# Gate differences taken on 128 partitions, prefix products in two scans, swapped rows put right at the copy of x, and a new order: an mLSTM with two MLP layers on Trainium2

## The chip, the cores and the metric

The kernel runs on one core of one Trainium2 chip. The metric is the device time of one execution in microseconds (us); the median of three runs is given with their lowest and highest. The engines are called PE (TensorE), VectorE (DVE in rows), ScalarE (ACT), GpSimd (POOL) and SyncE (SP, which issues the DMA transfers).

## The reference

Two batches of eight heads with 768 tokens each pass through a recurrent attention (an mLSTM), and its output, as 1536 rows of 320, through two MLP layers with a width of 2048. Everything is to be computed with the accuracy of fp32; the weights of the layers arrive as 64-bit floats.

```python
def _attn_ref(q, k, v, i_gate, f_gate, o_gate):
    ...
    for t in range(S):
        m_new = np.maximum(f_gate[:, :, t] + m, i_gate[:, :, t])
        f_stab = np.exp(f_gate[:, :, t] + m - m_new)
        i_stab = np.exp(i_gate[:, :, t] - m_new)
        m = m_new
        C = f_stab[:, :, None, None] * C + i_stab[:, :, None, None] * np.einsum('bhd,bhe->bhde', vt, kt)
        n = f_stab[:, :, None] * n + i_stab[:, :, None] * kt
        ...
        y[:, :, t] = o * h_tilde / denom
def _moe_ref(x, w_in, w_out):
    h = x @ w_in
    g = h * np.clip(h + 3.0, 0.0, 6.0) / 6.0
    return g @ w_out
def _moe2_ref(x, w_in, w_out):
    h = x @ w_in
    g = h * np.tanh(np.log1p(np.exp(h)))
    return g @ w_out
```

## The kernel before, in words

**Attention.** The 768 tokens are cut into six chunks of 128, each in two halves of 64. `scan_gates` computes the running maximum m for 16 rows (batch and head) by a scan on VectorE (L662) and then, by an addition and two subtractions on the same 16 partitions (tile `gio`; L309 is the helper that every operation on two tensors goes through), the arguments of the two exponentials; it runs for chunk 0, for chunk 1 (its three operations on POOL or VectorE, as the table `pool_scan` says) and for chunks 2 to 5 at once. `gates(c)` transposes the two results to 128 partitions by PE (bank `pg`), and ScalarE and VectorE make the exponentials from two sigmoids (tiles `ist` and `s`). Then it transposes the forget gates to 16 rows, and takes their prefix products over each half by a scan of 128 columns (tile `pr`), for which the first column of each half is copied to `first` and set to zero. `decays` (tile `fb`, two scans of 512 columns per chunk), `scores`, `cross`, `carry` and `within` are the matrix parts. `loads` brings the queries and keys of a chunk (`qke`, one buffer) and its keys, values and output gates (`kvo`). `mixture` ends a chunk: normalising, the output-gate product (`kvo<-fb,kvo`), two "tail" copies on ScalarE (L1034), PE's transposes into bank `xp`, and ScalarE's copies to `x`, the input of the first MLP layer: a rounded part (L1050) and the rest (L1056 or a subtraction on VectorE). For the second batch the two halves of a chunk stand in swapped order in the 128 rows, from `within` to the output.

**Layers.** Each product of the MLP layers is made in three products of high and low parts (`wh`, `wl`, `wd` of the weights, `gh`, `gl` of the activations). The weights of one slice are loaded in 64 bits (`ri` for the up part, `ro` for the down part, four buffers), narrowed to fp32 by a copy on ScalarE (`top`) and an integer operation on VectorE (L367), and split into high and low part by ScalarE and one of VectorE, POOL or PE (bank `pw`, `minus`). Layer 1 (`step1`, `step1_wide`) uses banks `ph` and `acc`, layer 2 (`step2`) `qh` and `bcc`, in three blocks of 512 columns. `store` copies an output tile from its bank and stores 128 rows of 320; for the second batch it does so in two transfers of 64 rows each (L1090), which puts the halves right.

**The order.** All of this is written as tasks that a planner (`Flow`) runs at build time: each step names its engine and a cost, and among those that could start next the one with the lowest number of the table `P` is recorded first. So the order on each engine is fixed when the kernel is built. Where PE would wait by the planner's model, it is given a "filler", a product of zeros into bank `pz` (`keep_warm`, L1200); these end when the first input of layer 1 is there.

```python
                while self.fill and place.free + 0.45 < first:
                    self.fill()
```

## Time and profile before

| | |
|---|---|
| median of 3 runs | 436.15 us (435.48 to 436.67) |
| the profiled execution | 436.73 us, span 435.0 us |
| mean granted clock of PE | 0.999 |
| PE busy | 426.3 us (98%) |
| VectorE busy | 303.9 us (70%) |
| ScalarE busy | 268.5 us (62%) |
| POOL busy | 60.8 us (14%) |
| chain that ended last | PE 87%, VectorE 5%, ScalarE 3% |

The chain is the work followed back from the last instruction, each step to what released it. A busy engine in this table is one with an instruction in flight; fillers count as busy for PE.

### The profile page before, as it was taken

The page shows a single profiled execution, that of the slowest core. Times are in us where ns is not written, and L with a number is a line of the kernel's source. Part 1 is how long each engine was busy: PE and PEld are TensorE (multiplying, and loading weights), DVE is VectorE, ACT ScalarE, POOL GpSimd, SP SyncE. Part 2 cuts the span into 40 slices and gives each one's busy share as a digit, 9 for nine tenths or more (in the row PEclk, how much of TensorE's full clock was granted, in tenths as well). Part 3 has the DMA queues.
Part 4 walks back from the last instruction along what each step waited for, and adds up shares of the span by engine and source line. Part 5 has one row for each costly group of instructions (what it writes and reads, how often), then busy time and mean ns, then how long its engine had stood idle before and what let it go on. Part 6 is the DMA issues. An engine that isn't in the chain of part 4 may idle for free.

```text
span 435.0 us, 9071 instructions
## 1 busy us (share of the span) xinstructions
PE 426.3 (98%) x3779; PEld 369.3 (85%) x3779; DVE 303.9 (70%) x532; ACT 268.5 (62%) x472; POOL 60.8 (14%) x54
## 2 busy tenths in 40 slices
PE   8999899999999999999999999999999999999995
PEld 6877899999988888787767788999999999899994
DVE  4999999999787323538976557666666666666673
ACT  5666676643533434169887357766676666766673
POOL 4030101270310135023045210000000000000000
PEclk9999999999999999999999999999999999999999
DMA  8966753552602035002772000000020000100002
GB/s 281 380 252 277 274 172 95 178 197 57 231 2 99 0 130 228 4 1 68 261 263 73 2 0 2 0 2 0 2 60 1 2 0 2 46 17 0 2 0 60
DMA packets 10136, 40.44 MB, mean 93 GB/s; under 512 B 2224, under 2 KB 3920, under 8 KB 9328
## 3 DMA queue, kind: packets, MB, share of 16 engines
q1 hardware_dynamic: 10096, 39.87, 25.9%
q8 instruction: 29, 0.48, 0.5%
q14 instruction: 11, 0.09, 0.1%
HBM read 37.64 MB, written 2.23 MB: 92 GB/s over the span
## 4 chain that ended last, share of the span: by engine, by line
PE 87%; DVE 5%; ACT 3%; issue 1%; DMA 1%; POOL 1%; DVEq 0%; POOLq 0%; ACTq 0%
PE qh L465 20%; PE accw L482 10%; PE phw L465 10%; PE acc L482 7%; PE ph L465 7%; PE bcc L1169 6%; PE bcc L1168 6%; PE bcc L1167 6%; PE pz L1200 4%; PE s L815 1%; PE st L942 1%; PE x L890 1%; PE z L985 1%; DMA ro<-in_w2o 1%; DVE ri L367 1%
## 5 line engine op out<-in xcount | busy, mean ns | idle before, releaser
L465 PE MATMUL qh<-x,wh 128*128 128x512 f32 x288 | 89.5, 392 | 0.0
L1118 DVE SCALAR_TENSOR_TENSOR u<-u,qh 128x512 f32<-128x512 f32 (+1 forms) x49 | 33.1, 675 | 39.0 <-ACT u L1116 39.0
L465 PEld LDWEIGHTS qh<-x,wh 128*128 128x128 f32 x288 | 52.3, 188 | 8.7
L1169 PE MATMUL bcc<-wd,gl 128*128 128x320 f32 x192 | 59.4, 309 | 0.2 <-DVE gl L1124 0.2
L1168 PE MATMUL bcc<-wd,gh 128*128 128x320 f32 x192 | 59.3, 309 | 0.0
L1167 PE MATMUL bcc<-wd,gh 128*128 128x320 f32 x192 | 59.3, 309 | 0.0
L465 PE MATMUL phw<-x,wh 128*128 128x512 f32 x192 | 58.9, 393 | 0.0
L1114 ACT ACTIVATE u<-u,two 128x512 f32<-128x512 f32 (+1 forms) x49 | 35.0, 715 | 30.9 <-DVE u L1112 30.7
L482 PE MATMUL accw<-ghw,wd 128*128 128x512 f32 x160 | 53.6, 400 | 0.0
L549 DVE SCALAR_TENSOR_TENSOR rw<-rw,phw 128x512 f32<-128x512 f32 x32 | 21.9, 685 | 38.4 <-ACT rw L547 38.3
L465 PEld LDWEIGHTS phw<-x,wh 128*128 128x128 f32 x192 | 35.7, 188 | 8.0
L482 PE MATMUL accw<-glw,wd 128*128 128x512 f32 x96 | 38.7, 403 | 0.5 <-POOL glw L309 0.4
L547 ACT ACTIVATE rw<-phw,half 128x512 f32<-128x512 f32 x32 | 22.0, 687 | 26.1 <-PE phw L465 26.0
L465 PE MATMUL qh<-x,wl 128*128 128x512 f32 x96 | 37.9, 395 | 0.0
L1167 PEld LDWEIGHTS bcc<-wd,gh 128*128 128x128 f32 x192 | 36.1, 188 | 2.1
L1168 PEld LDWEIGHTS bcc<-wd,gh 128*128 128x128 f32 x192 | 36.1, 188 | 1.9
L1108 ACT ACTIVATE u<-qh 128x512 f32<-128x512 f32 (+1 forms) x49 | 28.6, 586 | 14.4 <-PE qh L465 14.3
L1169 PEld LDWEIGHTS bcc<-wd,gl 128*128 128x128 f32 x192 | 36.1, 188 | 0.4 <-DVE gl L1124 0.4
L1124 DVE SCALAR_TENSOR_TENSOR gl<-u,gh 128x512 fp32r<-128x512 f32 (+1 forms) x49 | 33.0, 674 | 3.4 <-ACT gh L1122 3.3
L482 PEld LDWEIGHTS accw<-ghw,wd 128*128 128x128 f32 x160 | 29.5, 188 | 6.7 <-ACT ghw L552 0.5
L1112 DVE SCALAR_TENSOR_TENSOR u<-u 128x512 f32<-128x512 f32 (+1 forms) x49 | 33.4, 681 | 1.6
L465 PE MATMUL ph<-x,wh 128*128 128x256 f32 x192 | 34.2, 288 | 0.0
(153 smaller groups left out, 839.9 us busy)
## 6 DMA issues: line engine op xcount, KB each, us to landing
ri<-in_w1i SPq DMA_DIRECT2D x8, 768.0 KB, 6.0
qke<-in_qk SPq DMA_DIRECT2D x6, 1024.0 KB, 5.4
ri<-in_w2i SPq DMA_DIRECT2D x8, 768.0 KB, 5.5
kvo<-in_kvon SPq DMA_DIRECT2D x6, 968.0 KB, 7.8
ro<-in_w1o SPq DMA_DIRECT2D x8, 640.0 KB, 4.7
ro<-in_w2o SPq DMA_DIRECT2D x8, 640.0 KB, 5.3
fb<-fzd SPq DMA_DIRECT2D x4, 512.0 KB, 4.5
out<-ot SPq DMA_DIRECT2D x6, 160.0 KB, 1.8
```

The source lines that it names most:

```text
L465: T.matmul(ph, a, b, start=(i == 0), stop=(i == len(seq) - 1))
L482: T.matmul(acc[k], a, b, start=start, stop=stop, skip_group_check=True)
L547: A.activation(r, ph, AF.Relu, bias=half, scale=1.0 / 6.0)
L549: V.scalar_tensor_tensor(out=r, in0=r, scalar=1.0, in1=ph, op0=ALU.min, op1=ALU.mult)
L1108: A.activation(u, ph, AF.Exp)
L1112: V.scalar_tensor_tensor(out=u, in0=u, scalar=2.0, in1=u, op0=ALU.add, op1=ALU.mult)
L1114: A.activation(u, u, AF.Ln, bias=two)
L1118: V.scalar_tensor_tensor(out=u, in0=u, scalar=0.5, in1=ph, op0=ALU.subtract, op1=ALU.mult)
L1124: V.scalar_tensor_tensor(out=gl, in0=u, scalar=-2.0, in1=gh.bitcast(F32), op0=ALU.mult, op1=ALU.subtract)
L1167: T.matmul(acc, a, hi, start=st, stop=False)
L1168: T.matmul(acc, a, lo, start=False, stop=False)
L1169: T.matmul(acc, b, hi, start=False, stop=sp)
```

## The change

- **Gates.** `scan_gates` only scans. `gates(c)` transposes four pieces of 16 columns (forget gate, input gate, the maximum before and after) instead of two; ScalarE copies the two maxima out of the bank, VectorE adds and subtracts on 128 partitions (two operations), and the sigmoids read that result.
- **Prefix products.** Each half is scanned by itself, from 1.0 and with a tile of zeros (`nothing`), without the copy, the memset and the tile `first`.
- **Queries and keys of chunk 1** are loaded into the storage of the second block's x, on 16 rings, without a wait for the buffer of chunk 0; x of that block is made after chunk 1 has ended.
- **Swapped rows.** For the second batch ScalarE's copies to x read the two halves in reversed order. From there on the rows stand in the order of the output, and every tile is stored by one transfer of 128 rows. Of the last block, the second tile is copied by VectorE, the fourth by VectorE and ScalarE in two halves, the others by ScalarE.
- **Order and planner.** All priorities in `P` are new (one row shown), as are constants of the planner's model (the price of a filler, of a switch of PE's mode, of a transfer). The recorded program has 35 fillers instead of 61 before the first product of layer 1.

```diff
--- before.py
+++ after.py
 P = {
...
-    "gates": [81, 93, 41, 162, 127, 206],
+    "gates": [155, 42, 26, 201, 293, 59],
...
-    "pool_scan": [1, 0],
...
-    TO_PE, SWITCH = 0.13, 0.12
+    TO_PE, SWITCH = 0.13, (0.12, 0.21)
     TICK, COLUMNS = 10.24 / 3, 4000
-    DMA = dict(rings0=2.0, slow=13e3, fast=20e3, until=3.0, start=1.9, end=0.5)
+    FILL = 0.25
+    DMA = dict(first=1.5, rate=24e3, start=1.7, end=0.9)
...
-                    place.free = self.products(place.free, 0.214, 512)
+                    place.free = max(place.free + self.FILL, self.products(place.free, 0.214, 512))
                 mode = r[3] if len(r) > 3 else 0
-                start = first + (self.SWITCH if mode != self.mode else 0.0)
+                start = first + (self.SWITCH[mode > 0] if mode != self.mode else 0.0)
                 self.mode = mode
...
-    for j in range(len(BLOCKS) - 1):
-        new_x()
+    new_x()
...
-    first = gpool.tile([16, L], F32, tag="first", name="first")
+    nothing = gpool.tile([16, HL], F32, tag="nothing", name="nothing")
...
 def scan_gates(i, c0, c1):
...
-        on = i and P["pool_scan"][i - 1]
-        eng = G if on else V
-        for o, x, y, op in ((fgt, fgt, mt[:, a:z], ALU.add), (igt, igt, mt[:, a + 1 : z + 1], ALU.subtract),
-                            (fgt, fgt, mt[:, a + 1 : z + 1], ALU.subtract)):
-            yield flow.elementwise(on, 0.06 + 0.14 * n, 128 * n)
-            tt(eng, o[:, r], x[:, r], y, op)
         flow.set(scanned[i])
...
 def gates(c):
...
-        yield PE, 0.21, 128
-        T.transpose(p[:, 0:16], fgt[:, q], ident[:16, :16])
-        T.transpose(p[:, 16:32], igt[:, q], ident[:16, :16])
+        yield PE, 0.4, 256
+        for i, x in enumerate((fgt[:, q], igt[:, q], mt[:, q], mt[:, c * L + 1 : (c + 1) * L + 1])):
+            T.transpose(p[:, 16 * i : 16 * i + 16], x, ident[:16, :16])
         g = istab[c] = gpool.tile([128, 32], F32, tag=f"ist{c}", name=f"ist{c}")
         s = gpool.tile([128, 32], F32, tag=f"s{c}", name=f"s{c}")
-        yield ACT, 0.16
-        A.activation(s, p[:, 0:32], AF.Sigmoid, scale=-1.0)
-        A.activation(g, p[:, 0:32], AF.Sigmoid)
+        yield ACT, 0.1
+        A.copy(s, p[:, 32:64])
+        yield DVE, 0.08
+        tt(V, p[:, 0:16], p[:, 0:16], s[:, 0:16], ALU.add)
+        yield DVE, 0.1
+        tt(V, g.rearrange("t (x r) -> t x r", x=2), p[:, 0:32].rearrange("t (x r) -> t x r", x=2),
+           s[:, 16:32].unsqueeze(1).to_broadcast([128, 2, 16]), ALU.subtract)
         flow.put(in_a)
+        yield ACT, 0.25
+        A.activation(s, g, AF.Sigmoid, scale=-1.0)
+        A.activation(g, g, AF.Sigmoid)
         yield DVE, 0.27
...
-        begins = pr.rearrange("r (a t) -> r a t", a=2)
-        yield DVE, 0.08, True
-        V.tensor_copy(first.rearrange("r (a t) -> r a t", a=2)[:, :, 0:1], begins[:, :, 0:1])
-        yield DVE, 0.03, True
-        V.memset(begins[:, :, 0:1], 0.0)
-        yield DVE, 0.33, True
-        V.tensor_tensor_scan(out=pr, data0=pr, data1=first, initial=0.0, op0=ALU.mult, op1=ALU.add)
+        for a in range(2):
+            half_of = pr[:, a * HL : (a + 1) * HL]
+            yield DVE, 0.2, True
+            V.tensor_tensor_scan(out=half_of, data0=half_of, data1=nothing, initial=1.0, op0=ALU.mult, op1=ALU.add)
...
-        ends = begins[:, :, HL - 1]
+        ends = pr.rearrange("r (a t) -> r a t", a=2)[:, :, HL - 1]
...
 def loads(c, before):
...
-        yield in_qke
-        t["qke"] = apool.tile([128, B, 2, 4, L], F32, tag="qke", name=f"qke{c}")
-        yield SP, 852e3, ev["qk"], 13, 0.54
+        if c == 1:
+            flat = xpool.tile([128, 3072], F32, tag="x1", name="qke1")[:, 0 : 16 * L]
+            t["qke"] = flat.rearrange("p (b y h t) -> p b y h t", b=B, y=2, h=4)
+        else:
+            yield in_qke
+            t["qke"] = apool.tile([128, B, 2, 4, L], F32, tag="qke", name=f"qke{c}")
+        yield SP, 1049e3, ev["qk"], 16, 0.5
         SY.dma_start(out=t["qke"], in_=qk[c])
         t["ring"] = in_x2 if c in (1, 3) else in_kvo
...
-        flow.put(in_qke)
+        if c != 1:
+            flow.put(in_qke)
...
 def mixture(c):
...
             if c // 2 == len(X):
-                yield ends[3]
+                yield ends[1 if c // 2 == 1 else 3]
                 new_x()
             xcol = ((c % 2) * 2 + b) * L
             xh, xl = (z[:, :, xcol : xcol + L] for z in X[c // 2])
             ps = xp[:, 0:384].rearrange("p (k t) -> p k t", k=3)
+            if b:
+                ps, xh, xl = (z.rearrange("p k (a t) -> p k a t", a=2) for z in (ps, xh, xl))
+                xh, xl = xh[:, :, ::-1], xl[:, :, ::-1]
             yield ACT, 0.37
             A.copy(xh, ps)
...
 def store(j, k):
...
-        on_dve = j == len(BLOCKS) - 1 and k % 2
-        if on_dve:
+        acc, last = acc_l2[j, k][:, 0:DM], j == len(BLOCKS) - 1
+
+        def half():
+            yield ACT, 0.24
+            A.copy(ot[:, 160:DM], acc[:, 160:DM])
+
+        if last and k == 3:
+            other = flow.add(P["drain"][9], half())
+            yield DVE, 0.24
+            V.tensor_copy(ot[:, 0:160], acc[:, 0:160])
+            yield other
+        elif last and k == 1:
             yield DVE, 0.41
-            V.tensor_copy(ot, acc_l2[j, k][:, 0:DM])
+            V.tensor_copy(ot, acc)
         else:
             yield ACT, 0.33
-            A.copy(ot, acc_l2[j, k][:, 0:DM])
+            A.copy(ot, acc)
         flow.put(in_acc2)
-        for a in range(2) if b else (None,):
-            yield SP, 82e3 if b else 164e3, (ev := Event()), 16, 0.35
-            t0 = b * S + c * L
-            if b:
-                SY.dma_start(out=out[t0 + a * HL : t0 + a * HL + HL, :], in_=ot[64 - 64 * a : 128 - 64 * a])
-            else:
-                SY.dma_start(out=out[t0 : t0 + L, :], in_=ot)
+        t0 = b * S + c * L
+
+        yield SP, 164e3, (ev := Event()), 16, 0.35
+        SY.dma_start(out=out[t0 : t0 + L, :], in_=ot)
...
 def clear():
...
-        G.memset(first, 0.0)
+        G.memset(nothing, 0.0)
```

On VectorE, the last operations up to the first chunk's gate product `kvo<-fb,kvo`, the number in a tile's name being its place in the program. Before:

```order
L309 TENSOR_TENSOR oc_107<-x_0_455,px_292 64x164 x2
L309 TENSOR_TENSOR oc_107<-x_1_456,px_292 64x164 x2
L367 SCALAR_TENSOR_TENSOR ro_4_318<-ro_4_318,top_92 128x640
L367 SCALAR_TENSOR_TENSOR ro_2_328<-ro_2_328,top_91 128x640
L309 TENSOR_TENSOR fb_105<-z_0_488,oc_107 128x2x164
L309 TENSOR_TENSOR fb_105<-z_0_489,oc_107 128x2x164
L1020 TENSOR_SCALAR rc_531<-fb_105 128x16
L1022 SCALAR_TENSOR_TENSOR rc_531<-fb_105,rc_531 128x16
L1024 RECIPROCAL rc_531<-rc_531 128x16
L309 TENSOR_TENSOR kvo_158<-kvo_158,rc_531 128x640
L367 SCALAR_TENSOR_TENSOR ri_1_333<-ri_1_333,top_92 128x768
L309 TENSOR_TENSOR kvo_158<-fb_105,kvo_158 128x640
```

Now:

```order
L308 TENSOR_TENSOR kvo_180<-kvo_180,ist_407 128x656
L308 TENSOR_TENSOR fb_104<-z_0_415,oc_106 128x2x164
L712 SCALAR_TENSOR_TENSOR pr_478<-pr_478,nothing 16x64
L1021 TENSOR_SCALAR rc_450<-fb_104 128x16
L842 SCALAR_TENSOR_TENSOR fb_105<-fb_0_459,eye 128x512
L1023 SCALAR_TENSOR_TENSOR rc_450<-fb_104,rc_450 128x16
L712 SCALAR_TENSOR_TENSOR pr_478<-pr_478,nothing 16x64
L1025 RECIPROCAL rc_450<-rc_450 128x16
L308 TENSOR_TENSOR dd_523<-cst,pr_478 16x16
L308 TENSOR_TENSOR kvo_153<-kvo_153,rc_450 128x640
L366 SCALAR_TENSOR_TENSOR ro_3_193<-ro_3_193,top_91 128x640
L308 TENSOR_TENSOR kvo_153<-fb_104,kvo_153 128x640
```

Two narrowings of `ro` and one of `ri` no longer stand among these, while operations of the second chunk's gates (`pr`, `dd`, `ist`, `fb_105`) stand between those of the first.

On ScalarE, from the tail copies (L1034 before, L1035 now) to the last copy of x (L1050 and L1056 before, L1054 and L1060 now). Before:

```order
L405 CAST wh_1_114<-ri_1_333 128x768
L1034 COPY kvo_158<-kvo_158 128x2x2x32
L398 CAST wd_2_113<-pw_2_320_564 128x64
L398 CAST wd_2_113<-pw_2_320_564 128x256
L1034 COPY kvo_158<-kvo_158 128x2x2x32
L1050 CAST x_93<-xp_0_616 128x3x128
L1056 CAST x_93<-xp_0_616 128x3x128
L1050 CAST x_93<-xp_0_631 128x3x128
L864 ACTIVATE kvo_532<-kvo_532 128x640
L1056 CAST x_93<-xp_0_631 128x3x128
```

Now, from just behind the tail copies and the casts of `wd_3`:

```order
L847 COPY ul_573<-fb_105 128x16
L1054 CAST x_93<-xp_0_568 128x3x128
L416 CAST wd_4_127<-ro_4_240 128x2x320
L1060 CAST x_93<-xp_0_568 128x3x128
L397 CAST wd_3_118<-pw_3_320_575 128x64
L397 CAST wd_3_118<-pw_3_320_575 128x256
L364 CAST top_92<-ri_2_392 128x768
L1054 CAST x_93<-xp_0_590 128x3x2x64
L397 CAST wd_4_127<-pw_4_320_584 128x64
L397 CAST wd_4_127<-pw_4_320_584 128x256
L416 CAST wd_1_109<-ro_1_361 128x2x320
L1060 CAST x_93<-xp_0_590 128x3x2x64
```

More casts of `wd` and a narrowing copy of `ri_2` stand between the copies of x; the copies of the second batch have their columns in two halves (3x2x64).

On SP, the last stores, `ot_k` being the tile of the k-th 128 rows of a block. Before:

```order
L1090 DMA out<-ot_3_4408 64x320 x2
L1092 DMA out<-ot_0_4857 128x320
L1090 DMA out<-ot_1_4862 64x320 x2
L1092 DMA out<-ot_2_4868 128x320
L1090 DMA out<-ot_3_4871 64x320 x2
```

Now:

```order
L1103 DMA out<-ot_3_4382 128x320
L1103 DMA out<-ot_0_4842 128x320
L1103 DMA out<-ot_1_4847 128x320
L1103 DMA out<-ot_2_4853 128x320
L1103 DMA out<-ot_3_4856 128x320
```

Each tile is one transfer.

## Rows read from the trace of the kernel before

**Rows 1.** Stretches: length, busy us of PE, PEld, VectorE, ScalarE, POOL; clock, DMA, GB/s

```profile
5.30:33.80 28.50, 28.50 (x472) 22.00 (x474) 25.85 (x57) 18.67 (x41) 5.12 (x5) 1.00 0.85 332
50.00:100.00 50.00, 48.86 (x679) 46.80 (x679) 48.37 (x98) 31.87 (x67) 12.66 (x10) 1.00 0.51 166
```

**Rows 2.** Timeline of PE: start, us, engine, line, operation, count [idle before]

```profile
8.71 0.23 PE L679 MATMUL pg<-eye,gio 16*128 16x16 f32 x1
...
8.93 1.66 PE L1200 MATMUL pz<-zeros 128*128 128x512 f32 x6
...
39.08 0.50 PE L465 MATMUL ph<-x,wh 128*128 128x256 f32 x2
```

**Rows 3.** Groups of PE to 39.08 us: count, busy us, mean ns, idle before

```profile
L1200 PE MATMUL pz<-zeros 128*128 128x512 f32 x61 | 19.8, 460 | 1.3 <-POOL zeros L1197 1.3
```

**Rows 4.** Timeline of VectorE: gate product of the first chunk

```profile
32.92 0.82 DVE L309 TENSOR_TENSOR kvo<-fb,kvo 128x640 f32<-128x640 f32 x1
```

**Rows 5.** Groups of VectorE to 39 us

```profile
L842 DVE TENSOR_TENSOR_SCAN fb<-fb,eye 128x512 f32<-128x512 f32 x4 | 4.9, 1216 | 0.7 <-PE fb L840 0.7
L367 DVE SCALAR_TENSOR_TENSOR ro<-ro,top 128x640 uint32<-128x640 uint32 x5 | 4.0, 811 | 0.7 <-ACT top L365 0.7
L367 DVE SCALAR_TENSOR_TENSOR ri<-ri,top 128x768 uint32<-128x768 uint32 x3 | 2.8, 938 | 0.0
...
L309 DVE TENSOR_TENSOR wd<-ro,wd 128x128 fp32r<-128x128 f32 (+1 forms) x4 | 2.1, 555 | 0.1
L309 DVE TENSOR_TENSOR kvo<-kvo,ist 128x656 f32<-128x656 f32 x2 | 1.7, 827 | 0.0
...
L309 DVE TENSOR_TENSOR wl<-ri,wh 128x512 fp32r<-128x512 f32 x2 | 1.4, 688 | 0.3 <-ACT wh L405 0.3
...
L309 DVE TENSOR_TENSOR wh<-ri,wh 64x256 fp32r<-64x256 f32 x2 | 0.8, 423 | 0.0
...
L309 DVE TENSOR_TENSOR gio<-gio,mt 16x128 f32<-16x128 f32 x3 | 0.8, 276 | 0.0
...
L309 DVE TENSOR_TENSOR ist<-ist,s 128x32 f32<-128x32 f32 x2 | 0.3, 174 | 0.1
```

**Rows 6.** Groups of ScalarE to 39.1 us

```profile
L365 ACT CAST top<-ri 128x768 f16<-128x768 bf16 x4 | 4.3, 1064 | 0.0
L417 ACT CAST wd<-ro 128x640 fp32r<-128x640 f32 x5 | 3.8, 785 | 1.8 <-DVE ro L367 1.8
L398 ACT CAST wd<-pw 128x64 fp32r<-128x64 f32 (+1 forms) x12 | 2.9, 291 | 1.0 <-PE pw L395 1.0
...
L1050 ACT CAST x<-xp 128x384 fp32r<-128x384 f32 x2 | 1.0, 480 | 0.7 <-PE xp L1041 0.7
```

**Rows 7.** Timeline of ScalarE, tail copies of the first chunk

```profile
33.87 0.29 ACT L1034 COPY kvo<-kvo 128x128 f32<-128x128 f32 x1
34.07 0.47 ACT L398 CAST wd<-pw 128x64 fp32r<-128x64 f32 x2
```

**Rows 8.** Timeline of PE, a wait ahead of a layer 1 down product

```profile
51.20 0.39 PE L482 MATMUL acc<-gl,wd 128*128 128x256 f32 x1 [1.14 <-DVE gl L309]
```

**Rows 9.** Timeline of VectorE ahead of that wait

```profile
48.39 1.58 DVE L309 TENSOR_TENSOR ist<-ist,s 128x32 f32<-128x32 f32 x1
```

**Rows 10.** Timeline of POOL ahead of that wait

```profile
48.25 1.68 POOL L309 TENSOR_TENSOR wd<-ro,wd 128x640 fp32r<-128x640 f32 x1 [18.22 <-ACT wd L417]
```

**Rows 11.** Groups of VectorE from 39 to 52 us

```profile
L309 DVE TENSOR_TENSOR gio<-gio,mt 16x512 f32<-16x512 f32 x3 | 2.0, 673 | 0.0
```

**Rows 12.** Timeline of VectorE, the last copy

```profile
429.85 0.49 DVE L1081 COPY ot<-bcc 128x320 f32<-128x320 f32 x1 [0.39 <-PE bcc L1169]
```

**Rows 13.** Timeline of SP's DMA queue, the last two stores

```profile
431.31 1.10 SPq L1090 DMA_DIRECT2D out<-ot  x2
```

**Rows 14.** DMA issues from 428 us: count, KB each, median us to landing

```profile
out<-ot SPq DMA_DIRECT2D x2, 160.0 KB, 1.9
out<-ot SPq DMA_DIRECT2D x4, 80.0 KB, 2.1
```

More of the change, by code (lines that the diff above doesn't have):

```diff
@@ L42 @@
 P = {
[L43 to L49 removed]
[4 rows of a table removed]
+    "const": [37, 163, 192],
+    "gates": [155, 42, 26, 201, 293, 59],
+    "load": [51, 158, 147, 234, 100, 142],
+    "score": [277, 8, 20, 32, 235, 273],
+    "value": [68, 57, 264, 128, 129, 244],
+    "carry": [174, 69, 181, 270, 75, 54],
+    "unit": [4, 91, 240, 38, 73, 62],
[4 rows of a table added]
     "up2": [
[3 rows of a table removed]
[3 rows of a table added]
     ],
     "down2": [
[L60 to L62 removed]
+        94, 81, 183, 22, 172, 27, 52, 187, 117, 43, 122, 66, 5, 48, 198, 114, 189, 13, 109, 134, 131, 86,
+        65, 169, 17, 24, 49, 16, 95, 197, 7, 162, 104, 219, 31, 186, 87, 0, 139, 176, 18, 141, 99, 67, 79,
+        15, 74, 97,
     ],
     "wide1": [
[L65 to L66 removed]
+        261, 223, 295, 173, 137, 206, 3, 160, 251, 126, 217, 247, 14, 281, 123, 98, 255, 274, 93, 232, 89,
+        150, 245, 200, 175, 170, 204, 289, 92, 144, 148, 218,
     ],
     "down1w": [
[L69 to L73 removed]
+        35, 107, 30, 212, 229, 249, 151, 119, 112, 120, 179, 288, 83, 34, 110, 210, 199, 125, 284, 111, 101,
+        135, 25, 276, 6, 64, 28, 140, 132, 195, 262, 283,
+    ],
+    "drain": [167, 127, 121, 102, 143, 146, 84, 203, 72, 130],
+    "now": [9, 11],
     "window": [0.05],
@@ L86 @@
     "pe_rest": [0, 0, 0, 0, 0, 1, 0, 1, 0, 1, 0, 0, 0, 0, 0, 0],
-    "pool_scan": [1, 0],
     "pe_low": [1, 1, 0, 0, 0, 0, 0, 0, 0, 0, 0, 0],
     "spread": [1, 1, 0, 0, 0, 0],
-    "decay": [182, 253, 178, 141, 158, 104],
-    "gload": [236, 40, 164, 175, 92, 181],
-    "cross": [163, 83, 258, 103, 238, 66],
-    "within": [214, 161, 36, 107, 112, 8],
+    "decay": [185, 56, 254, 76, 168, 215],
+    "gload": [105, 88, 44, 47, 85, 272],
+    "cross": [55, 53, 205, 220, 222, 177],
+    "within": [82, 106, 211, 269, 258, 71],
     "act_rows": [0, 0, 1, 0, 0, 1],
@@ L158, in __init__ @@
         self.now = 0.0
-        self.rings, self.landed = [2.0] * 16, []
+        self.rings, self.landed = [self.DMA["first"]] * 16, []
         self.tick, self.columns, self.fast = 0, 0.0, False
@@ L240, in transfer @@
         d = self.DMA
-        rate = d["slow"] if t < d["until"] else d["fast"]
         for i in range(n):
-            self.rings[i] = max(self.rings[i], t + d["start"]) + size / n / rate
+            self.rings[i] = max(self.rings[i], t + d["start"]) + size / n / d["rate"]
         end = max(self.rings[:n]) + d["end"]
@@ L1182, in start @@
         flow.add(P["now"][0], keep_warm())
-        yield SP, 16e3, (ev := Event())
+        yield SP, 64e3, (ev := Event())
         SY.dma_start(out=gio[:, :, 0:L], in_=gates_io[:, :, 0:L])
@@ L1238, in constants @@
     def constants():
-        yield SP, 7e3, have["cst"]
+        yield SP, 28e3, have["cst"]
         SY.dma_start(out=cst, in_=consts)
     def other_gates():
-        yield SP, 82e3, have["gates"]
+        yield SP, 328e3, have["gates"]
         SY.dma_start(out=gio[:, :, L:], in_=gates_io[:, :, L:])
```

15 lines of the change are left out of this document (removed), and 14 rows, old and new, of the table P.

## Prediction

> **What bounds the kernel now.** I read the busy shares first: PE is busy 98% of the span, so only what keeps PE off useful products can move the time. Then the stretches. In the opening PE looks full (28.50 of 28.50 us), but much of that is filler: 61 products of zeros, 19.8 us, 0.325 us each, issued so that PE is never idle [rows 1, 3]. The first useful product of the first layer starts at 39.08 us [rows 2]. What it waits for is VectorE, busy 25.85 of those 28.50 us [rows 1]: the first chunk's attention ends there with the output-gate product, 32.92 to 33.74 us [rows 4], and behind it stand ScalarE's two tail copies and the copies of x, with PE's transposes between. From then on PE is dense: from 50 to 100 us it misses 1.14 of 50 us, which is one wait, while VectorE is busy 48.37 us [rows 1, 8]. At the end the last copy ends at 430.34 us, and the last two stores are issued by SP from 431.31 us on, 0.55 us each [rows 12, 13].
>
> **The change part by part.** A measurement of this kernel tells a difference of about 0.3% (1.3 us) from none.
>
> *A. The opening.* Counted in VectorE's queue up to the gate product, the change has two fewer narrowings of `ro` (2 x 0.811) and one fewer of `ri` (0.938), because other weights come first, one fewer decay scan (1.216), and no gate subtractions (3 x 0.276). It has one more product of values and gate (0.827) and four short operations on 128 partitions, taken as the `ist` product (4 x 0.174). One pair of `wd` subtractions (2 x 0.555) gives way to one `wl` and one `wh` (0.688 + 0.423), which is equal [rows 5]. Sum: -4.60 + 1.52 = -3.1 us, so the gate product ends at about 30.6 instead of 33.74. The prefix products exchange a scan of 128 columns, a copy and a memset for two scans of 64; I take nothing, because VectorE's 2.65 idle us of the stretch [rows 1] can hold a difference of a few tenths; without that cover it is at most one short operation (0.174) more per chunk [rows 5].
>
> Behind the gate product the new order gives part of this back on ScalarE. Its two tail copies now stand behind a cast of `wd` (0.785) and a narrowing copy (at most 1.064) [rows 6]. If both are done by then they cost nothing, if neither, 1.85 us; I take the middle, 0.9, and start the copies at 31.5. Up to the last copy of x stand sixteen operations: three short copies (0.29 at most), six of `pw` (0.291), four copies of x (0.480), two casts of `wd` (0.785), one narrowing (1.064), together 7.2 us [rows 6, 7]. Neighbours overlap: the copy of 33.87 us lasts 0.29, the next starts at 34.07, so 0.09 less for each of fifteen, 5.9 us [rows 7]. The last copy of x ends at 37.4, PE starts 0.2 us later, at 37.6 instead of 39.08: **-1.5 us**. The bounds: nothing, where ScalarE's work neither overlaps nor was begun earlier (31.5 + 7.2 + 0.2 = 38.9), and -5.7, where all of VectorE's 3.1 us and its 2.65 idle us come back. I stand near the first, since ScalarE's rows fill that distance. The copies with reversed halves have no row; the nearest is the plain copy, 0.480 [rows 6], and at worst two of them double, +1.0. The earlier loads of the second chunk (its queries and keys go into the storage of a later x) move four weight loads behind them on SP; in the opening a DMA share of 0.85 [rows 1] leaves room for about 4 of 28.5 us, so I take nothing, and +1 as the bound.
>
> *B. The wait at 51.20 us.* PE waits 1.14 us for VectorE's `gl` [rows 8]. Ahead of it VectorE's `ist` product took 1.58 us [rows 9] instead of 0.174 [rows 5], at the time when POOL's `wd` subtraction ran from 48.25 for 1.68 us [rows 10]. VectorE loses three subtractions of 512 columns of 16 partitions there, 2.0 us together [rows 11], and gets two short operations for each of the coming chunks. I take **-0.9 us**; the bounds are 0 and -1.14. The Trainium skill, page "GPSIMD Engine Reference", section "1. Specifications", says that GpSimd's SBUF interface is shared with VectorE, with contention from VectorE's instructions with two SBUF inputs. The trace agrees, with 1.58 against 0.174 us. By this rule B could be nothing, since POOL keeps subtractions of this kind in the change and merely has them at other places; the total would be 0.9 us more.
>
> *C. Two more transposes per chunk.* A pair of them takes 0.22 us, from 8.71 to the next product at 8.93 [rows 2]. The pairs of the first two chunks fall among fillers; those of the other four stand among useful products: **+0.9 us**, bounds +0.4 and +0.9. The copy before and the two operations after them are on ScalarE and VectorE, with the next block's gates not due for tens of us.
>
> *D. The last stores.* For the swapped batch each tile leaves in two issues of 0.55 us [rows 13]; now one. The last four tiles need four issues instead of six. The last issue was at 431.31 + 0.55 = 431.86; with two fewer it would be 430.76, and 0.1 to 0.2 sooner since the last copy (0.49, ending at 430.34 [rows 12]) is shared by two engines. A transfer of 160 KB lands 1.9 us after its issue, one of 80 KB 2.1 [rows 14]. So 1.1 + 0.2: **-1.3 us**; bounds -0.5 (one issue saved, and no more) and -1.7.
>
> Sum: -1.5 - 0.9 + 0.9 - 1.3 = -2.8 us. Against the profiled execution (436.73 us, of which the span is 435.0) this gives 433.9; the median of the runs, 436.15, lies 0.6 below that execution, so I forecast 433.3 us.
>
> **The rivals.** *R1, the clock falls (slower).* Only 35 of 61 fillers are left. Before 39.08 us PE has 39.08 - 19.8 = 19.3 us for everything else, its waits counted in [rows 2, 3]; with 35 x 0.325 = 11.4 it has 30.7 of 37.6 us to do, and is idle for 6.9. In the trace before it is never idle in this stretch and the granted clock is 1.00 [rows 1]; what an idle PE is granted the rows don't show. Work at 1.2 instead of 2.4 GHz takes twice as long. So up to 6.9 us of work at the lower level the idle time absorbs the loss, and from 11.0 us on (4.1 more than that) the kernel is slower by 1.3 us than before. If it is half of the work, 15.4 us, the first product comes 8.5 us later than I say: A is +7.0, the time 436.15 + 7.0 - 1.3 = 441.9. For it: the fillers were there and are fewer. Against it: the idle time comes in pieces, with attention products between, and the fillers that stay lie mainly at the start. The Trainium skill, page "TensorE: Matmul & The Clock Gate", section "Part 1: The HAM clock gate", has the clock set by how busy PE has been recently; no run here shows it fall.
>
> *R2, VectorE takes A and B back (no change).* It is busy 48.37 of 50 us from 50 to 100 us [rows 1]: weights narrowed later in the opening are narrowed here, and a PE that arrives earlier waits for them. Three narrowings (2 x 0.811 + 0.938 = 2.56 [rows 5]) against A and B (2.4) would do. Then C and D are left: 436.15 + 0.9 - 1.3 = 435.75. Against it: the stretch holds one wait now.
>
> *R3, all of the opening comes back (faster).* The narrowing and casts on ScalarE are done in time and VectorE's idle time goes too: A is -5.7, the time 436.15 - 5.7 - 1.3 = 429.2. Against it: sixteen operations on ScalarE.
>
> *R4, the weights' loads are late, or POOL's contention stays (faster, less).* A or B is nothing: 434.2 to 434.8. That the stores don't merge is no rival: the order has one transfer for each tile.
>
> **How the numbers follow.** Forecast 0.55, R4 0.11, R2 0.15, R3 0.08, R1 0.11. Faster by over 0.3% are the forecast, R4 and R3: 0.74; within 0.3%: R2, 0.15; slower: R1, 0.11. The forecast's own range, from its bounds taken half together, is 431.3 to 434.8. The range 430.5 to 435.9 takes in R4 and R2 and leaves out R1 and R3, 0.19.
>
> **What would show it.** Right: the gate product ends near 30.6, the first product of layer 1 starts near 37.6 us, the clock is 1.00 in the opening with PE not full, no wait of over 0.5 us between 50 and 100 us, four transposes in about 0.45 us, five single stores at the end with the last issue some 1.1 us nearer to the last matmul. Wrong: a granted clock well below 1 before 35 us (R1), waits for `gl` or for weights on PE between 40 and 100 us that add up to over 2 us (R2), a first product before 35 us (R3).

## The result, and the profile after

The changed kernel takes 441.23 us (median; 440.41 to 442.49). Beside it the kernel before takes 435.95 us (435.48 to 436.67). The ratio is 1.0122, with a 95% interval of 1.0093 to 1.0151: 1.2% slower, where 433.3 us was forecast, and outside the range (430.5 to 435.9). The profiled execution took 441.46 us. Its page begins with the span, the busy shares and the chain that ended last:

```profile
span 439.4 us, 9016 instructions
...
PE 422.4 (96%) x3765; PEld 366.5 (83%) x3765; DVE 302.0 (69%) x532; ACT 269.6 (61%) x479; POOL 61.8 (14%) x51
...
PE 64%; DVE 14%; ACT 8%; DMA 8%; issue 3%; POOL 1%; SPq 0%; DVEq 0%; ACTq 0%; POOLq 0%
```

PE is busy 96% instead of 98%, and VectorE has 14% of the chain instead of 5%, ScalarE 8% instead of 3%. The next view gives stretches of the changed kernel, with the columns of [rows 1]: up to the first product of layer 1 (39.80 us), from there to the last product, and three pieces.

```profile
0.00:39.80 39.80, 32.19 (x568) 25.38 (x568) 28.93 (x65) 22.39 (x50) 2.91 (x10) 0.96 0.79 300
39.80:435.70 395.90, 390.19 (x3200) 341.16 (x3198) 272.78 (x467) 246.90 (x429) 58.93 (x41) 1.00 0.20 70
5.30:33.80 28.50, 22.21 (x478) 17.47 (x477) 24.08 (x55) 15.93 (x36) 0.00 (x0) 1.00 0.88 348
22.00:27.20 5.20, 3.96 (x110) 2.97 (x109) 4.59 (x14) 2.47 (x7) 0.00 (x0) 1.00 1.03 416
33.60:37.00 3.40, 3.40 (x12) 2.59 (x10) 3.40 (x7) 2.31 (x8) 0.00 (x0) 0.50 0.12 18
```

The same view of the kernel before, for the corresponding long stretch and for the piece from 22.0 us:

```profile
39.08:429.90 390.82, 388.86 (x3193) 340.76 (x3190) 272.43 (x466) 244.18 (x421) 52.69 (x39) 1.00 0.20 70
22.00:27.20 5.20, 5.20 (x112) 4.03 (x112) 5.07 (x10) 2.17 (x4) 0.63 (x1) 1.00 0.35 131
```

This gives the balance. The opening ends 0.72 us later than before, not 1.5 sooner; in the stretch of [rows 1] PE is idle for 6.3 us, and was for none. In the kernel before the last product ends at 429.80 us, so the stretch shown runs on 0.1 us behind it. From the first product of layer 1 to the last product PE needs 395.9 us instead of 390.7, 5.2 more: it is idle 5.7 us instead of 1.9 (+3.8), and busy 1.3 us more, with 3200 products against 3193. From the last product to the end of the span it is 439.4 - 435.7 = 3.7 us, and was 435.0 - 429.8 = 5.2: -1.5. Sum: 0.7 + 5.2 - 1.5 = 4.4, the difference of the spans.

**The opening.** The timeline of VectorE and ScalarE at the first chunk's gate product and tail copies ([rows 4, 7] before):

```profile
30.59 0.82 DVE L308 TENSOR_TENSOR kvo<-fb,kvo 128x640 f32<-128x640 f32 x1
...
32.16 0.48 ACT L1035 COPY kvo<-kvo 128x128 f32<-128x128 f32 x2
```

The gate product ends at 31.41 us instead of 33.74, and the tail copies start at 32.16. I had said 30.6 and 31.5. The timeline of PE behind that:

```profile
29.52 0.36 PE L721 MATMUL pf<-eye,pr 16*128 16x8 f32 x2
32.06 0.28 PE L723 MATMUL pf<-eye,pr 16*64 16x8 f32 x4 [2.18 <-issue]
...
32.84 0.73 PE L393 MATMUL pw<-ro,eye 128*128 128x320 f32 x2
...
34.55 1.27 PE L393 MATMUL pw<-ro,eye 128*128 128x320 f32 x2
...
39.80 0.28 PE L463 MATMUL ph<-x,wh 128*128 128x256 f32 x1
```

PE stands still for 2.18 us ahead of a transpose of the prefix products (L723), and the releaser is "issue": nothing that the profile shows is waited for. Then the granted clock is 0.50, the lower level (1.2 GHz), from 33.6 to 37.0 us, and the pair of products of the weights' split takes 1.27 us where the same pair ahead of that stretch took 0.73. The loads are the other thing that differs here. In the stretch 22.0 to 27.2 us the DMA engines are full (1.03), where before they were at 0.35. DMA activity of the changed kernel by queue (packets, MB, share of 16 engines), first from 27.2 to 29.7 us, then from 29.7 to 31 us:

```profile
q1 hardware_dynamic: 151, 1.03, 98.5%
...
q8 instruction: 1, 0.02, 5.1%
```

The instruction queue moves nothing from 27.2 to 29.7 us, and then one packet, which the trace has from 29.74 to 30.80 us; PE goes on 1.26 us after its end. This is the mark that the experiments follow.

**Behind the opening.** The longest of PE's waits from 38 us on (total, times, longest):

```profile
PE x L890 <- DVE c L308: 1.5, 1, 1.5
PE accw L480 <- DVE glw L308: 1.0, 1, 1.0
PE acc L480 <- POOL gl L308: 0.8, 1, 0.8
PE accw L480 <- POOL glw L308: 0.6, 1, 0.6
```

The wait for `gl` at 51.20 us [rows 8] is gone, as was said. These are new. They stand further back: from 40 to 100 us PE is idle for 1.0 us, but from 100 to 160 us for 2.4 and from 225 to 240 us for 2.0, where it was idle for none before. The timeline around the first two of them:

```profile
150.78 2.07 POOL L308 TENSOR_TENSOR glw<-rw,ghw 128x512 fp32r<-128x512 f32 x1 [3.72 <-ACT ghw L550]
...
151.71 1.50 DVE L308 TENSOR_TENSOR c<-c,pe 104x328 f32<-104x328 f32 x1
...
153.84 0.50 DVE L308 TENSOR_TENSOR c<-c,pe 104x328 f32<-104x328 f32 x1
...
153.87 0.33 PE L890 MATMUL x<-c,qke 40*64 40x41 f32 x8 [1.54 <-DVE c L308]
...
230.14 1.29 POOL L308 TENSOR_TENSOR wl<-ri,wh 128x512 fp32r<-128x512 f32 x1
...
230.30 1.69 DVE L308 TENSOR_TENSOR glw<-rw,ghw 128x512 fp32r<-128x512 f32 x1 [0.69 <-ACT ghw L550]
...
232.04 0.50 PE L480 MATMUL accw<-glw,wd 128*128 128x512 f32 x1 [0.99 <-DVE glw L308]
```

VectorE's sum `c` takes 1.50 us beside POOL's subtraction `glw`, and 0.50 when POOL is still (at 153.84 us). Its `glw` takes 1.69 beside POOL's `wl`; undisturbed a subtraction of this size takes 0.69 [rows 5]. It is the mechanism of [rows 9, 10] at other places. The other two waits are for POOL itself. Its `gl` at 100.93 us takes 1.73 us beside a subtraction of VectorE, its `glw` at 233.88 us takes 1.28, which is what POOL takes for this size at most places (1.28 to 1.30). So that last wait is POOL's own length, nearly twice VectorE's 0.69, and no collision.

**The end.** SP's queue and the landing of the last stores ([rows 13, 14] before):

```profile
434.87 1.93 SPq L1103 DMA_DIRECT2D out<-ot  x4
...
out<-ot SPq DMA_DIRECT2D x4, 160.0 KB, 1.8
```

Four issues in 1.93 us, where the last four tiles took six.

### The profile page after: what moved, and what is told of

The parts are those of the page before. It is cut to its first block, busy times and chain, and to the rows that moved or that the text cites. A ratio compares the mean times of both kernels' runs of the same rounds, so it can differ in the third digit from the quotient of the medians.

```text
span 439.4 us, 9016 instructions
## 1 busy us (share of the span) xinstructions
PE 422.4 (96%) x3765; PEld 366.5 (83%) x3765; DVE 302.0 (69%) x532; ACT 269.6 (61%) x479; POOL 61.8 (14%) x51
## 4 chain that ended last, share of the span: by engine, by line
PE 64%; DVE 14%; ACT 8%; DMA 8%; issue 3%; POOL 1%; SPq 0%; DVEq 0%; ACTq 0%; POOLq 0%
PE qh L463 18%; PE accw L480 10%; PE phw L463 9%; PE bcc L1180 6%; PE bcc L1179 5%; PE bcc L1178 5%; DMA gio<-in_gates_io 3%; PE acc L480 3%; PE ph L463 2%; DVE fb L842 2%; DMA ri<-in_w2i 2%; DVE c L308 1%; DVE ri L366 1%; DVE kvo L308 1%; ACT top L364 1%
## 5 line engine op out<-in xcount | busy, mean ns | idle before, releaser
L1129 DVE SCALAR_TENSOR_TENSOR u<-u,qh 128x512 f32<-128x512 f32 (+1 forms) x49 | 33.1, 675 | 37.6 <-ACT u L1127 37.6
L1125 ACT ACTIVATE u<-u,two 128x512 f32<-128x512 f32 (+1 forms) x49 | 35.0, 715 | 30.7 <-DVE u L1123 30.6
L1119 ACT ACTIVATE u<-qh 128x512 f32<-128x512 f32 (+1 forms) x49 | 28.5, 585 | 12.7 <-PE qh L463 12.6
L545 ACT ACTIVATE rw<-phw,half 128x512 f32<-128x512 f32 x32 | 22.0, 688 | 22.5 <-PE phw L463 22.2
L463 PE MATMUL ph<-x,wh 128*128 128x256 f32 x192 | 35.1, 290 | 0.1
L1133 ACT ACTIVATE gh<-u 128x512 fp32r<-128x512 f32 (+1 forms) x49 | 30.3, 618 | 6.9 <-DVE u L1129 6.8
```

The costliest lines, as they stand in the source:

```text
L463: T.matmul(ph, a, b, start=(i == 0), stop=(i == len(seq) - 1))
L545: A.activation(r, ph, AF.Relu, bias=half, scale=1.0 / 6.0)
L1119: A.activation(u, ph, AF.Exp)
L1125: A.activation(u, u, AF.Ln, bias=two)
L1129: V.scalar_tensor_tensor(out=u, in0=u, scalar=0.5, in1=ph, op0=ALU.subtract, op1=ALU.mult)
L1133: A.mul(gh, u, -2.0)
```

## The experiments

Theory: the loss comes from (1) a full DMA that brings PE's instructions late, (2) the low clock behind that stall, and (3) POOL and VectorE in each other's way at new places; the stores are a gain. The rivals: the clock alone (few fillers), or the gates and the new products of the order themselves. Kernels x1 to x8 are edits of the changed kernel, b1 to b4 of the kernel before. The kernel before ran again beside each of them, with medians from 436.25 to 436.98 us, so kernels are compared by their ratios to it.

**x1: the third chunk's queries and keys are loaded later.**

```diff
-        SY.dma_start(out=t["qke"], in_=qk[c])
+        if c == 2:
+            held.append(lambda: SY.dma_start(out=t["qke"], in_=qk[c]))
+        else:
+            SY.dma_start(out=t["qke"], in_=qk[c])
...
+        if not c:
+            G.tensor_copy(out=tiles[2]["qke"][0:1, 0, 0, 0, 0:1], in_=t["tail"][0:1, 255:256])
+            held.pop()()
```

> The changed kernel, with the load of chunk 2's queries and keys (1 MB, issued at 22.5 us) held back until the first chunk's tail copies are done, by a copy of one element on POOL that the transfer has to wait for; the order on every engine stays. Theory 1: PE's 2.18 us without work from 29.9 us is a late fetch of PE's own instructions, which stands behind data that keeps the DMA engines full to 31 us. Then the fetch comes sooner, the stall falls below 0.5 us, the clock stays at 1.00 to 40 us, the first product of layer 1 starts at 37.3 to 38.0 instead of 39.80, and the time falls by at least 2 us, to 439 or less. If the waits between 47 and 235 us (5 us more than before) also come from the late opening (theory 2), the time is 434 to 436. If they belong to the new order itself (rival to theory 2), it is 438 to 439.5. Rival to theory 1: the stall has another cause; it stays, and the time is 441.

443.49 us (440.59 to 446.69), ratio 1.0124 [1.0076, 1.0171]. PE's timeline and two stretches (columns as above):

```profile
44.37 0.43 PE L895 MATMUL x<-c,qke 40*64 40x41 f32 x15 [2.24 <-issue]
...
10.00:22.00 12.00, 10.91 (x165) 9.00 (x167) 8.87 (x18) 5.70 (x13) 0.00 (x0) 0.58 1.01 398
45.00:53.00 8.00, 8.00 (x110) 7.46 (x102) 5.43 (x17) 5.03 (x14) 0.00 (x0) 0.57 0.65 256
```

The second piece of the edit stands in `mixture`, behind the first chunk's tail copies, from which the held load waits by one element that POOL writes. The stall at 30 us is gone and one of 2.24 us stands at 44 us, where the held load now fills the DMA engines (1.03 from 39.5 to 42.2 us). So it goes with the load, and again an instruction packet ends (at 43.08 us) 1.29 us before PE goes on. The time is no better: the low clock came behind the stall, and in this execution also for most of 10 to 22 us, where no stall stands ahead of it, only a pause of 2.29 us in which PE waits for VectorE's `ist`.

**x2: twelve more fillers** ahead of the first two chunks' gate transposes.

```diff
+        for _ in range(7 - 2 * c if spread else 0):
+            flow.fill()
```

> The changed kernel with twelve more fillers on PE, seven ahead of the first chunk's transpose of the gates to rows and five ahead of the second chunk's; everything else as it is. Rival R1 (fewer fillers let the clock fall): PE has no gaps over 0.5 us at 9 and 24 us, the clock stays at 1.00 to 40 us and the first product starts some 1 us sooner, time about 440. Theory 1 (late instruction fetch): the stall of 2.2 us near 30 us stays, since PE needs as many instructions by then and a few more, the clock falls behind it as now, and the time is 441 within 1 us.

442.83 us (440.90 to 445.27), ratio 1.0134 [1.0089, 1.0178]. PE's waits and one stretch:

```profile
PE fb L842 <- issue: 2.4, 1, 2.4
...
33.60:37.00 3.40, 3.40 (x12) 2.51 (x10) 2.79 (x5) 1.22 (x5) 0.00 (x0) 0.50 0.00 0
```

The pauses at 9 and 24 us were filled, the stall stayed (2.4 us) and with it the low clock behind it; the first product of layer 1 comes at 40.86 us. Fillers do not reach the cause of the stall.

**x3: two stores for each swapped tile** of the changed kernel.

```diff
-        SY.dma_start(out=out[t0 : t0 + L, :], in_=ot)
+        if b:
+            for a in range(2):
+                SY.dma_start(out=out[t0 + a * HL : t0 + a * HL + HL, :], in_=ot[a * HL : a * HL + HL])
```

> The changed kernel, with the second batch's tiles stored in two transfers of 64 rows each, in the order in which the rows now stand. If the single transfers are worth what part D says, this is 1.3 us slower than the changed kernel, 442.5, the end lies 5.0 us or more behind the last product instead of 3.7. If the transfers are hidden, the time is 441.2.

444.34 us (443.14 to 444.79), ratio 1.0161 [1.0124, 1.0198]. The last product ends at 437.45 us and the span at 442.5: 5.1 us, against 3.7. The stores are worth 1.4 us. By the ratios x3 lies 1.7 us above the changed kernel, by the medians 3.1; what is not the stores lies ahead of them, where the clock was low from 8.6 to 12 and from 32.5 to 39.3 us.

**b1: only the stores**, in the kernel before: swapped rows at the copy of x, one transfer for each tile.

```diff
+            if b:
+                ps, xh, xl = (z.rearrange("p k (a t) -> p k a t", a=2) for z in (ps, xh, xl))
+                xh, xl = xh[:, :, ::-1], xl[:, :, ::-1]
...
+        SY.dma_start(out=out[t0 : t0 + L, :], in_=ot)
```

> The kernel before with one part of the change alone: swapped rows put right at the copies to x, and one transfer per stored tile; order, gates and scans as before, the last copies whole. Part D predicts 1.1 to 1.3 us less than before, 434.7, with the end 4.0 us behind the last product instead of 5.2, if copies with reversed halves take the 0.48 us of plain ones. If they take twice as long, A gives back up to 1 us and the time is about 435.7.

434.33 us (433.75 to 435.95), ratio 0.9943 [0.9920, 0.9965]: 0.6% faster, clear of noise. SP's queue:

```profile
429.25 1.84 SPq L1091 DMA_DIRECT2D out<-ot  x4
```

From the last product (430.08 us) to the end 3.6 us. The first product of layer 1 starts at 39.32 us, 0.24 later than in [rows 2]: the copies with reversed halves cost no more than that, and take 0.48 us each in this trace, as plain ones do.

**x4: five of POOL's subtractions go to VectorE**, those that stand beside the new waits.

```diff
-            tt(ei, wl, ...
+            tt(V if nm == "1_7" else ei, wl, ...
-        tt(G if P["pool_low"][i] else V, gl, ...
+        tt(G if P["pool_low"][i] and i not in (13, 21, 22, 40) else V, gl, ...
```

> The changed kernel, with five of POOL's subtractions done by VectorE at the same places of the order: the low parts gl of step 13 and glw of steps 21, 22 and 40, and wl of the last slice of layer 2, those that run at 100.9, 145.6, 150.8, 233.9 and 230.1 us. Theory 2b: PE's waits at 102, 152, 230 and 235 us (4.0 us together) come from VectorE and POOL holding each other up, since VectorE's operations beside them take 1.0 to 1.1 us longer than elsewhere. Then these waits fall below 2 us together, and the time by about 2 to 3, to 438 to 439. Rival: VectorE's queue is simply full there; with 0.7 us more for each of five operations the waits stay or grow, and the time is 441 to 443.

438.48 us (435.65 to 440.22), ratio 1.0020 [0.9987, 1.0053]. One of PE's waits from 38 us on, and the stretch from the first product of layer 1 to the last product:

```profile
PE x L890 <- DVE c L308: 0.5, 1, 0.5
...
40.48:433.40 392.92, 390.09 (x3200) 341.28 (x3198) 270.93 (x473) 246.99 (x430) 52.69 (x36) 1.00 0.20 71
```

The waits for `gl`, `glw` and 1.0 of the 1.5 us for `c` are gone, and a wait of 0.8 us for ScalarE's `ghw` is new. The stretch takes 392.9 us instead of 395.9: the five moves bring 3.0 us (2.7 by the medians, 4.4 by the ratios). They take away the collisions and POOL's longer time for the same work together, and do not tell one from the other. The opening is no better: first product at 40.48 us, with a stall of 1.36 us and the clock low from 11.8 to 22.0 us.

**x5: x1 and x2 together.**

> The changed kernel with both edits of the first two experiments: chunk 2's queries and keys held back until the first chunk's tail copies, and twelve more fillers. Theory 1 with R1: the late fetch and the fall of the clock behind gaps of PE are two separate losses of the opening. With both taken away there is no stall over 0.5 us and no lower clock up to 40 us, the first product starts at 37.3 to 38.3 us, and the time falls to 438 to 439.5, the waits after 45 us being left. Rival: the first product stays at 39.5 or later, since VectorE and ScalarE set it, and the time is 441.

442.03 us (440.05 to 445.31), ratio 1.0130 [1.0093, 1.0167]. PE's timeline and two stretches:

```profile
41.01 0.32 PE L897 MATMUL x<-c,qke 40*64 40x41 f32 x7 [1.29 <-issue]
...
5.00:40.00 35.00, 32.30 (x595) 24.80 (x594) 30.82 (x65) 22.39 (x52) 1.64 (x2) 1.00 0.81 312
44.00:47.40 3.40, 3.40 (x16) 3.23 (x16) 3.25 (x14) 2.28 (x7) 0.00 (x0) 0.50 1.01 402
```

The opening is as forecast (clock 1.00, first product at 37.81 us), but the held load meets PE's next instructions at 41 us (DMA engines at 1.02 from 39 to 41 us, an instruction packet that ends at 39.73), and the low clock follows. By 51 us the gain is gone.

**b2: the kernel before with 34 of its 61 fillers.**

```diff
+            filled[0] += 1
+            if filled[0] <= 21 or filled[0] % 3 == 0:
                 T.matmul(pz, zeros[:, 0:128], zeros, start=True, stop=True)
```

> The kernel before with 34 of its 61 fillers (the first 21, then each third); all else as it is. R1: PE has gaps in the opening, the clock falls to 1.2 GHz for parts of it, and the first product starts 1 to 3 us later than 39.08, time 437 to 439, with more spread from run to run. Rival (A, VectorE alone sets the opening): the gaps cost nothing, the clock stays, the time is 436 as before or up to 1 us less.

435.89 us (434.26 to 440.24), ratio 0.9983 [0.9949, 1.0017]. One stretch, and PE's timeline:

```profile
23.00:32.00 9.00, 8.97 (x172) 6.91 (x170) 8.08 (x16) 6.09 (x11) 2.06 (x2) 0.62 0.56 219
...
39.27 0.51 PE L465 MATMUL ph<-x,wh 128*128 128x256 f32 x2
```

The clock does fall (0.62 on average over 9 us), and the first product comes 0.19 us later. Fewer fillers alone lose nothing in the median of the old order; that PE's work there waits for VectorE anyway is my reading of it. Two of the ten executions, with the lowest granted clock (0.983 and 0.984 over the whole), took 438.39 and 440.24 us, so a longer fall may cost more; the kernel before reached 440.09 us beside them, so this is not shown.

**b3: only the gates**, in the kernel before: L669 taken out; four transposes, a copy and two operations on 128 partitions put in, as in the change's diff.

> The kernel before with the change's gates alone, in the old order: no subtractions on 16 partitions, four transposes for each chunk, differences on 128 partitions; prefix scans, loads and stores as before. Part C predicts 0.7 to 0.9 us more on PE for the last four chunks, part A 0.8 us less on VectorE in the opening, part B some of the wait of 1.14 us at 51 us. The sum is 435 to 436. If the four transposes wait for the copy and the two operations behind them in queues that were laid out for two, the time is 437 or more.

439.25 us (437.27 to 441.00), ratio 1.0051 [1.0023, 1.0078]: 0.5% slower, clear of noise. The timeline around 51 us:

```profile
50.30 1.87 POOL L309 TENSOR_TENSOR wd<-ro,wd 128x640 fp32r<-128x640 f32 x1 [18.85 <-DVE ist L309]
...
50.74 1.98 DVE L309 TENSOR_TENSOR gl<-r,gh 128x512 fp32r<-128x512 f32 x1
...
52.77 0.39 PE L482 MATMUL acc<-gl,wd 128*128 128x256 f32 x1 [1.11 <-DVE gl L309]
```

The first product comes at 40.54 us, 1.46 later than in [rows 2]. The wait of [rows 8] stays, 1.11 us: it is VectorE's `gl` itself that now runs beside POOL's `wd`, for 1.98 us.

**x6: the opening and the collisions together**: x2's fillers, x4's five moves, and the load of x1 held only until the first chunk's normalisers are done (`in_=rc[0:1, 0:1]`), so that it ends sooner.

> The changed kernel with the repairs together: chunk 2's queries and keys held back only until the first chunk's normalisers are done (some 29 us, when the loads ahead of them have landed), the twelve more fillers, and the five subtractions of POOL on VectorE. If the causes found (late fetch of instructions, clock behind gaps, VectorE and POOL holding each other up) are the loss, the first product starts at 37.5 to 38.5, the waits at 102, 152, 230 and 235 us stay small as with the five moves alone, and the time is 434 to 436.5, that is 2 to 4 us below the moves alone in the part before 60 us. If the second fetch stall, at 41 to 44 us, stays, it is 437 to 438.

435.94 us (435.33 to 436.51), ratio 0.9983 [0.9957, 1.0010]. The long stretches, and the DMA queues from 27.2 to 29.7 us:

```profile
0.00:37.67 37.67, 34.48 (x579) 26.54 (x580) 28.80 (x64) 22.04 (x50) 3.67 (x11) 1.00 0.84 316
37.67:430.30 392.63, 389.70 (x3200) 341.19 (x3198) 271.42 (x473) 246.86 (x430) 52.64 (x36) 1.00 0.21 71
...
q1 hardware_dynamic: 55, 0.25, 24.1%
q8 instruction: 1, 0.02, 2.7%
```

The first product of layer 1 starts at 37.67 us, the clock is 1.00, and the instruction packet is there before 29.7 us, with the other loads at 24% instead of 98%. Behind it PE is idle 2.9 us instead of 5.7. The last product ends 5.4 us sooner than in the changed kernel: the whole loss is back, though not the gain that was forecast. Against the kernel before, the opening is 1.4 us shorter and the end 1.6, but the stretch between them still takes 392.6 us instead of 390.7.

**x7: the changed kernel with the old gates** (three operations on 16 partitions on VectorE, two transposes).

> The changed kernel with the gates as before: the three operations on 16 partitions behind each scan, all on VectorE, two transposes for each chunk instead of four, and no copy and differences on 128 partitions; the order of the rest stays. If the new gates cost time on their longer path (the old order with them took 2.7 us more), this is 1 to 2.5 us faster than the changed kernel, 439 to 440. If they save VectorE's time where it is the bound, it is 1 to 2 us slower, 442 to 443, the wait for VectorE near 47 to 50 us growing by the 2.0 us that the three operations of 512 columns take.

444.17 us (441.87 to 444.49), ratio 1.0152 [1.0092, 1.0211]. PE's waits:

```profile
PE pg L675 <- DVE gio L308: 1.4, 2, 1.1
```

With the old gates the transposes wait for `gio` (1.4 us), and the time is 2.9 us longer by the medians, 1.3 by the ratios. But the intervals of x7 and of the change overlap, and the profiled execution of x7 has the lower clock in two more stretches (12.6 to 16.0 and 46.8 to 50.2 us). So what the new gates are worth in the new order is not shown, not even its sign; in the old one b3 has them slower.

**x8: x6 without the twelve fillers.**

> The kernel with all repairs, without the twelve extra fillers. If the clock that falls behind PE's gaps is a loss of its own (R1), the lower clock comes back in the opening, by 3.4 or 6.8 us or more in some executions, the runs scatter over 3 us or more instead of 1.2, and the median is 1 to 3 us higher, 437 to 439. If the late fetch and the blocking of VectorE and POOL were all, the time stays at 435.9 within 0.7 us, with the same spread.

436.35 us (435.66 to 438.06), ratio 0.9989 [0.9963, 1.0014]. One stretch of the profiled execution (438.04 us):

```profile
10.00:22.00 12.00, 11.24 (x185) 9.32 (x186) 8.75 (x18) 5.57 (x13) 0.00 (x0) 0.57 1.02 402
```

There the first product comes at 39.66 us, 2.0 later than in x6. No stall stands ahead of the fall; PE pauses there for 2.24 us ahead of 10.76 us, where x6 with its fillers pauses for 0.20. Yet six of twelve executions took 435.7 to 436.2 us, with a granted clock of 0.996 or more over the whole, and five took 437.2 to 438.1 with 0.992 or less: with the loads out of the way the clock costs about 2 us in those executions in which it falls, and little in the median.

**b4: b1, and two of POOL's subtractions on VectorE** (`wd` of slice 1_0, the one of [rows 10], and `glw` of step 38).

```diff
-                tt(eo, wd[:, :, 320:640], ...
+                tt(V if nm == "1_0" else eo, wd[:, :, 320:640], ...
-        tt(G if P["pool_low"][i] else V, gl, ...
+        tt(G if P["pool_low"][i] and i != 38 else V, gl, ...
```

> The kernel before with the part of the change that paid (swapped rows put right at the copy to x, one transfer per tile) and two of POOL's subtractions on VectorE: the wd of layer 2's first slice, which ran beside the operation of 1.58 us ahead of PE's wait at 51.20 us, and the glw of step 38, beside the wait at 222.9 us. Theory 2b: these waits (1.14 and 0.41 us) come from VectorE and POOL holding each other up, so they fall below 0.5 together, and the time is 1 to 1.5 us below the same without the two moves (434.33), 433.0. Rival: VectorE is full there, the waits stay, 434.3 or more.

433.67 us (432.77 to 437.26), ratio 0.9941 [0.9911, 0.9970]: faster than the kernel before and the changed one. VectorE's timeline:

```profile
48.09 0.17 DVE L309 TENSOR_TENSOR ist<-ist,s 128x32 f32<-128x32 f32 x1
...
48.75 0.69 DVE L309 TENSOR_TENSOR gl<-r,gh 128x512 fp32r<-128x512 f32 x1
```

`ist` takes 0.17 us instead of 1.58 [rows 9] and `gl` 0.69, and the wait of [rows 8] is gone. But by the ratios b4 lies only 0.1 us below b1 (0.9941 against 0.9943), by the medians 0.7, and the intervals overlap: that the two moves add a gain of their own is not shown, though a wait of 1.1 us went.

## Why the prediction was wrong

Two steps failed. By the stretches, the opening (A) was forecast at -1.5 us and came out at +0.7, what lies between (B and C) at 0 and came out at +5.2, the end (D) at -1.3 and came out at -1.5. So 2.2 us of the miss are the opening's, and 5.2 the stretch behind it.

**A, the opening: the failed step is "I take nothing, and +1 as the bound" for the earlier loads.** I asked only which weights would be late, and set bytes against an average DMA share of 0.85. But the second chunk's new storage frees the first chunk's buffer for the third chunk's load at 22.5 us, and the share from 22.0 to 27.2 us goes from 0.35 to 1.03. What came late were PE's instructions. x1, x5 and x6 move the load, and stall and packet move with it. Where PE stops says the same: in PE's records of each trace, counted from the first, the stalls of over 1 us with no releaser stand behind the 961st record (changed kernel, x2, x3, x4, x7) or the 1217th (x1, x5), which are 256 apart, whatever work follows, and in all seven PE goes on 1.2 to 1.5 us after the end of an instruction packet. The Trainium skill, page "Runtime: NRT & Kernel Launch", section "Instruction fetch mechanics", has instructions brought in blocks by a DMA queue and this mostly hidden; here it is not hidden, 2.18 us. The term came out at +0.7 instead of -1.5: 2.2 us, for the stall and the low clock behind it together.

VectorE's sum held as work and not as time: up to the gate product it is busy 22.8 us instead of 26.0, 3.2 less (3.1 was said), but idle 0.9 us more, and the product ends at 31.4 instead of 30.6. In x6, where the first product starts at 37.67 us (37.6 was said), it ends no sooner, at 31.71. That x6 hits the number is partly luck, as these rows of ScalarE and PE in x6 show:

```profile
37.53 0.55 ACT L1070 CAST x<-xp 128x384 fp32r<-128x384 f32 x1
...
38.13 0.38 PE L463 MATMUL ph<-x,wh 128*128 128x256 f32 x1 [0.18 <-ACT x L1070]
```

The last copy of x ends at 38.08 us, not at 37.4, and the first product, against my path, does not wait for it; a later one does. The 0.2 us that I put between the two stand in no row.

**R1, the clock: partly right.** In the profiled execution of the changed kernel the clock was low for 3.4 us behind the stall, and more fillers did not prevent that (x2). But in five kernels without the twelve fillers (x1, x3, x4, x7, x8) it was also low in the opening before 23 us, with no stall ahead, and in the three with them (x2, x5, x6) it was not. x8 beside x6 gives the price, some 2 us where it falls. That is R1's way, and smaller than its size: R1 had the first product at 46.1 us (37.6 + 8.5), and it came at 39.80. That R1's time, 441.9, lies near the measured 441.23 is luck.

**B, the wait at 51.20 us: right for the place, wrong for the kernel.** The wait went, and PE is idle for only 0.2 us from 50 to 100 us. The failed step is that the worst case of B was the gain not made, 0.9 us; R4 has the same bound. PE's idle time behind the opening grew by 3.8 us, and five moved subtractions bring back 3.0 us of the stretch (x4). The Trainium skill, page "SBUF — State Buffer", section "SBUF: two separate sides", has the access that VectorE and GpSimd share as a lock for a whole instruction; the rows agree, with 1.50 against 0.50 us and 1.69 against 0.69. I took one known collision away and looked for no new ones, nor for subtractions left to POOL whose result PE needs soon, though the order of every instruction on both engines was to be had.

**R2** named waits of more than 2 us in all on PE between 40 and 100 us. They did not come: PE is idle there for 1.0 us. The idle time that grew lies behind, and not for narrowings put off.

**C, the transposes: mis-sized.** Two rows of PE in the changed kernel, the starts of two groups of four:

```profile
43.35 0.29 PE L672 MATMUL pg<-eye,gio 16*128 16x16 f32 x2
...
43.63 0.27 PE L672 MATMUL pg<-eye,gio 16*128 16x16 f32 x2
```

A chunk's four take 0.28 us, so the two added ones 0.14: about +0.6 for four chunks instead of +0.9, and within the 0.84 us by which PE is busier in x6 than before.

**D, the stores: right.** -1.5 us here, 1.4 in x3, 1.6 in b1; forecast -1.3.

**What stays open.** In the changed kernel PE is busy 1.3 us more than before, 0.5 of it more than x6; I put this down to restarts behind the waits, which no run shows alone. With all repairs (x6) the stretch behind the opening is still 1.9 us longer than before, and no run takes that apart beyond the 0.84 us of busy time. Why the new gates cost 1.46 us in the old opening (b3) isn't settled either; there VectorE's two operations were recorded at places that the planner had not chosen for them. One execution of each kernel is profiled, and where the clock falls differs between them.

## What to carry to other kernels

Price a transfer that moves forward by the DMA share of the stretch that it lands in, not by an average, and ask what else comes over those engines: an engine that runs through many small instructions needs its own code brought in time. When an order is made anew, look through the new one for two-input operations of VectorE and POOL side by side, because such a pair made one operation of VectorE 1.0 us longer here; and for results of POOL that PE needs at once. And a part that pays by itself, as the single stores here (0.57% alone), is worth taking without the rest.
